# A recurrent attention kernel: the Q/K and V work of each segment in finer pieces, and the projections of the extra tokens in 32-column tiles

## The chip, the cores and the metric

The kernel runs on one core of a Trainium2 chip. The metric is the device time of the core in microseconds (us). A time quoted for a kernel is the median of its runs. A run counts as slow when it lies over 1.5% above the fastest run of the same kernel, and the state is unknown for a kernel that ran only once. The chip also reports the clock that its throttle granted to the matmul engine, as a share of full speed.

The names of the engines in the profile are PE (matmuls), PEld (the load of the stationary operand of a matmul, which PE overlaps with other matmuls), DVE (the vector engine), ACT (the scalar engine), POOL (a general engine) and SP (which issues DMAs).

## The reference, cut to what matters

```python
# x: 2048 tokens of 512; 64 segments of 32 tokens; H = 32 heads of Dh = 128; 8 memory rows
mem = mem0
for s in range(64):
    h = concat([mem, x[32*s : 32*s+32]])         # 40 rows (x is layer-normalized)
    q, k, v = h @ Wq, h @ Wk, h @ Wv             # per head
    p = softmax(where(mask, q k^T * scale, -1e9))
    o = (p v) @ Wo                               # 40 x 512
    mem = o[:8]                                  # the next segment waits for this
    outs.append(o[8:])
h  = x + concat(outs)
h2 = h + B(layernorm(h))                         # a gated MLP with a 2048 x 2048 mix over the tokens
```

The line `mem = o[:8]` makes the 64 segments a recurrence: a segment can't start its projections before the output projection of the one before it is done.

## The kernel before

The kernel has three parts. A prologue loads the weights, normalizes the first tokens and computes projections ("X" in what follows) of the first "extra" tokens. These are the eight tokens of each segment that do not fit into the 32-row tiles in which the recurrence works. The loop runs the 64 segments, and pours the X projections of later segments into gaps of PE. The tail is the gated MLP.

The parts that the change touches, shortened:

```python
# Q and K of a segment: 2 halves of 16 heads x (Q, K), each 16 matmuls of 512 columns in 32-column tiles
def QK(s, b, mi):
    for dc in range(4):
        for c in range(4):
            matmul(ps[32*c:32*c+32, bank, :], lhsT=hT[:, sl, dc, :], rhs=<512 columns of w_q or w_k>, tile_position=(0, 32*c))
def QK_evac(s, b, mi):                      # PSUM -> SBUF on ACT, then a 32x32 block transpose on DVE
    act(activation(out=Tst[:, mi, :], in_=ps[:, bank, :]))
    dve(transpose(out=QT or KT, in_=Tst[:, mi, :]))

# X projections of Q and K: 16 full-array matmuls (128 x 128 x 128) to a group of four heads
def qkx_mm(ck, i, bank):
    for hh in range(4):
        for dc in range(4):
            matmul(ps[:, bank, hh*128:(hh+1)*128], lhsT=ws[:, dc, h*128:(h+1)*128], rhs=hTe[:, ck % 3, dc, :])

# the two normalization products of a half, both on DVE
def sm_norm(b):
    dve(scalar_tensor_tensor(E_sb[:, b, 0:160], R_sb, RK, E_sb))
    dve(scalar_tensor_tensor(<the 64 extra columns>, R_sb, RK, <the same>))

# order of one segment
for b in range(2):
    for mi in range(2): QK(s, b, mi); QK_evac(s, b, mi)
S_half(s, 0); sm_exp(0); V_half(s, 0); V_evac(0, "dve"); sm_sums(0); sm_ln(0)
S_half(s, 1); sm_exp(1); sm_rcp(0)
V_half(s, 1, (0, 1, 2)); sm_sums(1); sm_ln(1); sm_rcp(1); V_half(s, 1, (3,)); V_evac(1, "act")
sm_norm(0); sm_norm(1)
<one X group: matmuls>                       # filler
PV_half(s, 0); PV_half(s, 1); <evict the four banks>
<eviction of the X group>
Wo(...)                                      # 32 matmuls of 384 columns, then 32 of 128 columns
mem_out(s)                                   # the 8 memory rows, back to the input of the next segment
# [cut: gap fillers, DMA, the tail]
```

S is the score product, PV the product of the probabilities and V, and Wo the output projection.

The softmax here doesn't subtract the row's maximum and nothing guards it: scores larger than these inputs give would overflow.

## Time and profile before

The kernel before took 933.24 us as the median of three runs (933.03 to 933.27).

| what | us | read from |
|---|---|---|
| span of the profiled run | 931.4 | the profile page |
| prologue, to the first Q/K matmul of segment 0 | 33.04 | the timeline of PE |
| one segment, without X filler | 10.90 | the timeline of PE |
| one segment, with X filler | 10.95 to 11.0 in most | the timeline of PE |
| from the last segment's start to the end | 193.0 | the timeline of PE |

This is PE in segment 48 of the kernel before. Each line gives the start, the length, the engine, the source line, the operation, the operands, the shape, how many instructions, and in brackets the idle time before it with what ended it. L475 is Q/K, L505 the first matmuls of S, L586 PV, L619 Wo.

```profile
574.80 3.64 PE L475 MATMUL f_ps<-f_arena,f_hT 128*32 128x512 bf16 x64 [0.32 <-ACT f_hT L641]
578.26 0.27 PE L505 MATMUL f_ps<-f_mask,f_ident 128*32 128x224 bf16 x4
...
579.50 0.27 PE L505 MATMUL f_ps<-f_mask,f_ident 128*32 128x224 bf16 x4
...
582.05 0.28 PE L586 MATMUL f_ps<-f_E_sb,f_V_sb 32*128 32x40 bf16 x16 [0.56 <-DVE f_E_sb L560]
...
582.90 1.93 PE L619 MATMUL f_ps<-f_arena,f_cT 128*32 128x384 bf16 x64
...
585.70 0.61 PE L475 MATMUL f_ps<-f_arena,f_hT 128*32 128x512 bf16 x8 [0.30 <-ACT f_hT L641]
```

From one Q/K to the next are 585.70 − 574.80 = 10.90 us, and these are the steps: 3.46 to the first S, 3.79 from there to the second PV, 0.85 to Wo, 2.80 to the next Q/K. Before the second PV, PE waits 0.56 us for DVE (line 560, the product of the extra columns). Before Q/K it waits 0.30 us for ACT. A segment that also carries X filler takes only some 0.05 us more, so the filler fills gaps, and the segment is a chain of latencies.

In the prologue PE computes the X projections. This is the group of these matmuls in the kernel before, from the page's list of groups. Its columns are the shape (partitions by elements) and the count, then the busy time and the mean ns of one instruction, then the idle time before them and what ended most of it.

```profile
L406 PE MATMUL f_ps<-f_hTe,f_arena 128*128 128x128 bf16 x1024 | 66.8, 223 | 1.5 <-ACT f_V_sb L576 1.0
```

1024 matmuls had 1.5 us of idle time before them in the whole run, none of it worth naming in the prologue.

### The profile page before, as it was taken

How to read it: one execution, taken by the hardware profiler on the slowest of the kernel's cores; microseconds unless marked ns; L12 is line 12 of the kernel's file. 1: busy time of each engine (PE TensorE's matmuls, PEld its weight loads, DVE VectorE, ACT ScalarE, POOL GpSimd, SP SyncE). 2: the span in 40 equal slices, each digit the busy share in tenths (PEclk: the TensorE clock that was granted, in tenths of full speed). 3: DMA queues.
4: the chain of work that ended last, by engine and by line, in shares of the span. 5: the costliest groups of instructions: out<-in, count | busy, mean ns of one | idle time of the engine just before them, and what ended most of it. 6: DMA issues, size and time to landing. Idle time of an engine off the chain costs nothing.

```text
span 931.4 us, 45500 instructions
## 1 busy us (share of the span) xinstructions
PE 885.5 (95%) x20973; PEld 486.4 (52%) x20973; DVE 448.0 (48%) x1034; ACT 475.4 (51%) x1153; POOL 112.5 (12%) x280
## 2 busy tenths in 40 slices
PE   7979999999999999999999999998999999989998
PEld 6644555555555555555555555454444444444443
DVE  3434555555454555554545555444444464453434
ACT  2435666666565666666565656565656565500000
POOL 1511111111111111111101111111101022200000
PEclk9989999999999999999999999999999999999999
DMA  9952222122203211221213020413121292021201
GB/s 329 376 141 56 66 53 65 35 49 63 71 19 74 45 53 40 53 60 38 65 32 65 32 67 20 116 31 77 37 54 49 72 284 98 1 91 46 89 14 36
DMA packets 103380, 71.29 MB, mean 77 GB/s; under 512 B 62120, under 2 KB 88688, under 8 KB 103184
## 3 DMA queue, kind: packets, MB, share of 16 engines
q1 hardware_dynamic: 102672, 68.06, 25.8%
q8 instruction: 166, 2.72, 1.2%
q14 instruction: 30, 0.25, 0.1%
q0 software_dynamic: 192, 0.20, 0.1%
q10 hardware_dynamic: 320, 0.07, 0.0%
HBM read 39.46 MB, written 18.61 MB: 62 GB/s over the span
## 4 chain that ended last, share of the span: by engine, by line
PE 91%; ACT 4%; DVE 2%; issue 1%; DMA 1%; SPq 0%; POOL 0%
PE f_ps L475 25%; PE f_ps L619 13%; PE f_ps L569 11%; PE f_ps L1016 10%; PE f_ps L406 6%; PE f_ps L663 4%; PE f_ps L586 3%; PE f_ps L978 3%; PE f_ps L1009 3%; PE f_ps L1086 2%; PE f_ps L638 2%; PE f_ps L425 2%; PE f_ps L514 2%; ACT f_hT L641 1%; PE f_ps L535 1%
## 5 line engine op out<-in xcount | busy, mean ns | idle before, releaser
L475 PE MATMUL f_ps<-f_arena,f_hT 128*32 128x512 bf16 x4096 | 233.0, 380 | 10.5 <-ACT f_hT L641 8.0
L482 ACT ACTIVATE f_Tst<-f_ps 128x512 bf16<-128x512 f32 x256 | 152.8, 597 | 110.7 <-PE f_ps L475 110.1
L475 PEld LDWEIGHTS f_ps<-f_arena,f_hT 128*32 128x32 bf16 x4096 | 103.6, 97 | 122.0 <-ACT f_hT L641 24.1
L488 DVE STREAM_TRANSPOSE f_QT<-f_Tst 128x256 uint32<-128x256 uint32 x128 | 57.0, 445 | 176.6 <-ACT f_Tst L482 176.6
L569 PE MATMUL f_ps<-f_arena,f_hT 128*32 128x512 bf16 x2048 | 139.9, 378 | 0.0
L619 PE MATMUL f_ps<-f_arena,f_cT 128*32 128x384 bf16 (+1 forms) x4096 | 125.4, 275 | 2.4 <-ACT f_cT L605 2.1
L619 PEld LDWEIGHTS f_ps<-f_arena,f_cT 128*32 128x32 bf16 x4096 | 84.9, 97 | 61.0 <-ACT f_cT L605 31.4
L1016 PE MATMUL f_ps<-f_arena 128*128 128x512 bf16 x448 | 101.3, 379 | 2.5 <-DVE f_arena L1022 1.6
L631 ACT ACTIVATE f_part<-f_ps 128x384 bf16<-128x384 f32 (+1 forms) x128 | 46.4, 384 | 75.4 <-PE f_ps L619 75.4
L491 DVE STREAM_TRANSPOSE f_KT<-f_Tst 128x256 uint32<-128x256 uint32 x128 | 57.0, 445 | 52.8 <-ACT f_Tst L482 52.7
L607 DVE TENSOR_SCALAR f_cT<-f_ps 128x320 bf16<-128x320 f32 x128 | 56.9, 487 | 42.4 <-PE f_ps L592 42.4
L498 POOL COPY f_QT<-f_arena 128x256 bf16<-128x256 bf16 x64 | 30.8, 481 | 357.7 <-PE f_ps L520 357.6
L1016 PEld LDWEIGHTS f_ps<-f_arena 128*128 128x128 bf16 x448 | 43.5, 98 | 55.9 <-DVE f_arena L1022 2.6
L605 ACT ACTIVATE f_cT<-f_ps 128x320 bf16<-128x320 f32 x128 | 49.0, 435 | 39.4 <-PE f_ps L592 39.4
L406 PE MATMUL f_ps<-f_hTe,f_arena 128*128 128x128 bf16 x1024 | 66.8, 223 | 1.5 <-ACT f_V_sb L576 1.0
L406 PEld LDWEIGHTS f_ps<-f_hTe,f_arena 128*128 128x128 bf16 x1024 | 59.4, 100 | 11.2 <-issue 9.8
L555 DVE SCALAR_TENSOR_TENSOR f_E_sb<-f_R_sb,f_E_sb 128x160 bf16<-128x160 f32 x128 | 41.7, 326 | 46.0 <-ACT f_R_sb L551 46.0
L547 ACT ACTIVATE f_R_sb<-f_ps 128x160 f32<-128x160 f32 x128 | 38.8, 303 | 37.4 <-PE f_ps L540 37.4
L569 PEld LDWEIGHTS f_ps<-f_arena,f_hT 128*32 128x32 bf16 x2048 | 44.4, 95 | 21.8
L627 POOL COPY f_cTx<-f_cT 128x256 bf16<-128x256 bf16 x64 | 26.1, 408 | 196.8 <-DVE f_cT L607 196.8
L1022 DVE TENSOR_TENSOR f_arena<-f_ps,f_arena 128x512 f32<-128x512 f32 x28 | 19.3, 691 | 57.8 <-PE f_ps L1016 57.8
L586 PE MATMUL f_ps<-f_E_sb,f_V_sb 32*128 32x40 bf16 x2048 | 36.5, 178 | 10.5 <-DVE f_E_sb L560 9.0
(103 smaller groups left out, 1092.5 us busy)
## 6 DMA issues: line engine op xcount, KB each, us to landing
wT_d<-f_wst SPq DMA_DIRECT2D x32, 256.0 KB, 2.4
f_arena<-wT_d SPq DMA_DIRECT2D x32, 256.0 KB, 4.7
f_arena<-in_A_Wq_dram SPq DMA_DIRECT2D x4, 1024.0 KB, 9.7
f_arena<-in_A_Wk_dram SPq DMA_DIRECT2D x4, 1024.0 KB, 14.0
f_arena<-in_A_Wv_dram SPq DMA_DIRECT2D x4, 1024.0 KB, 14.5
f_arena<-in_A_Wo_dram SPq DMA_DIRECT2D x4, 1024.0 KB, 13.5
f_Vx<-vext_d SPq DMA_DIRECT2D x62, 64.0 KB, 2.5
vext_d<-f_Vs SPq DMA_DIRECT2D x24, 128.0 KB, 2.1
```

Source lines behind the costliest of these rows:

```text
L406: pe(lambda e, h=h, dc=dc, hh=hh: e.matmul(ps[:, bank, hh * 128:(hh + 1) * 128], lhsT=ws[:, dc, h * DH:(h + 1) * DH], rhs=hTe[:, ck % 3, d ...
L475: pe(lambda e, dc=dc, c=c, rhs=rhs: e.matmul(ps[32 * c:32 * c + 32, bank, :], lhsT=hT[:, sl, dc, :], rhs=rhs, start=(dc == 0), stop=(dc == ...
L482: act(lambda e: e.activation(out=Tst[:, tb, :].rearrange("p (hp i r) -> p hp i r", i=32, r=2), in_=ps[:, bank, :].rearrange("p (hp r i) -> ...
L488: dve(lambda e: e.transpose(out=dst, in_=src), reads=[("T", tb)], writes=[("QT", b)])
L491: dve(lambda e: e.transpose(out=dst, in_=src), reads=[("T", tb)], writes=[("KT", b)])
L569: pe(lambda e, dc=dc, c=c, c0=c0: e.matmul(ps[32 * c:32 * c + 32, bank, :], lhsT=hT[:, sl, dc, :], rhs=w_v[:, dc, c0:c0 + 512], start=(dc ...
L586: pe(lambda e, q=q, c=c, g=g, c0=c0: e.matmul(ps[:, PVB[c], c0:c0 + 40], lhsT=V_sb[q, b, g * 128:(g + 1) * 128], rhs=E_sb[q, b, g * 40:(g ...
L605: act(lambda e: e.activation(out=dst, in_=src, func=ACT.Copy, scale=UNSC), reads=[PB(PVB[c])], writes=[("cT", c)])
L607: dve(lambda e: e.tensor_scalar(out=dst, in0=src, scalar1=UNSC, scalar2=None, op0=ALU.mult), reads=[PB(PVB[c])], writes=[("cT", c)])
L619: pe(lambda e, h=h, g=g, i=i, b=b, c=c: e.matmul(ps[32 * g:32 * g + 32, bank, 0:d1 - d0], lhsT=cTh[:, i, 8:40], rhs=w_o[:, h, d0:d1], star ...
L631: act(lambda e: e.activation(out=part[:, s % 8, d0:d1], in_=ps[:, bank, 0:d1 - d0], func=ACT.Copy), reads=[PB(bank)], writes=[("part", s % ...
L1016: pe(lambda e: e.matmul(ps[:, bank, 0:TB], lhsT=z2[:, sc, fb * 128:(fb + 1) * 128], rhs=wTb[tb % 2][:, :, sc, :], start=(sc == 0), stop=(s ...
```

## The change

Its intent is to shorten the chain from Q/K to the second PV.

- The second half of Q and K comes in two 8-head pieces, so that the last eviction and transpose before the second S are half as long.
- The second half of V goes to two PSUM banks, each evicted on its own, one by DVE and one by ACT.
- The second S moves ahead of the sums of the first half and of the last quarter of V.
- The product of the extra columns moves from DVE to Pool, beside the other product.
- The X projections of Q and K use four 32-column tiles instead of the full array, so that PE does not change its mode between them and the matmuls of the segment. The first half of an X group goes before PV and the second half behind `mem_out`. One filler of V moves ahead of Wo.

The core of the diff, with cuts at "...":

```diff
-    def qkx_mm(ck, i, bank, only_hh=None, only_dc=None):
+    def qkx_mm(ck, i, bank, hhs=range(4)):
 ...
-                pe(lambda e, h=h, dc=dc, hh=hh: e.matmul(ps[:, bank, hh * 128:(hh + 1) * 128], lhsT=ws[:, dc, h * DH:(h + 1) * DH],
-                                                         rhs=hTe[:, ck % 3, dc, :], start=(dc == 0), stop=(dc == DC - 1)),
+                for c in range(4):
+                    q = slice(32 * c, 32 * c + 32)
+                    pe(lambda e, h=h, dc=dc, hh=hh, c=c, q=q: e.matmul(
+                        ps[q, bank, hh * 128:(hh + 1) * 128], lhsT=ws[:, dc, h * DH + 32 * c:h * DH + 32 * c + 32],
+                        rhs=hTe[:, ck % 3, dc, :], start=(dc == 0), stop=(dc == DC - 1), tile_position=(0, 32 * c)),
 ...
-    QKB = {(0, 0): 0, (0, 1): 1, (1, 0): 6, (1, 1): 7}
+    QKP = ((0, 0, 8, (0, 1)), (1, 0, 4, (6, 7)), (1, 4, 4, (3, 2)))     # (half, first pair, pairs, banks of Q and K)
-    VB = (6, 2)
+    VB = {(0, 0): 6, (1, 0): 2, (1, 1): 7}
 ...
     def sm_norm(b):
-        dve(lambda e: e.scalar_tensor_tensor(out=ev, in0=rv, scalar=RK, in1=ev, op0=ALU.mult, op1=ALU.mult),
+        pool(lambda e: e.tensor_tensor(out=ev, in0=rv, in1=ev, op=ALU.mult),
 ...
-        V_half(s, 0)
-        V_evac(0, "dve")
-        sm_sums(0)
-        sm_ln(0)
+        V_half(s, 0, (0, 1, 2))
         S_half(s, 1)
+        sm_sums(0)
         sm_exp(1)
+        sm_ln(0)
+        V_half(s, 0, (3,))
+        V_evac(0, "dve")
 ...
-        V_half(s, 1, (0, 1, 2))
+        V_half(s, 1, gs=(0, 2))
+        V_evac(1, "dve", (0, 2))
         sm_sums(1)
+        sm_rcp(0)
         sm_ln(1)
         sm_rcp(1)
-        V_half(s, 1, (3,))
-        V_evac(1, "act")
+        V_half(s, 1, gs=(2, 4))
+        V_evac(1, "act", (2, 4))
 ...
-        ev = [gx.pop(0)()] if gx else []
+        xs = gx.pop(0) if gx else []
+        for f in xs[:2]:
+            f()
         PV_half(s, 0)
         PV_half(s, 1)
 ...
-        late = []
+        late = gv.pour(1)
         Wo((0, 2, 1, 3), OB, 0, OC)
 ...
             mem_out(s)
-        late += gv.pour(1)
+        for f in xs[2:]:
+            f()
```

The scale constants of the softmax change too (a factor moved from one product into the eviction of V), and some groups of matmuls take another PSUM bank.

More of the change, by code (lines that the diff above doesn't have):

```diff
@@ L191, in fast_path @@
     NEG = -1.0e30
-    RBIAS = 44.42
+    RBIAS = 44.24
     LNS = 2.0 ** -64
-    RK = math.exp(-RBIAS)
+    VSC = 2.0 ** -64
     em = Emitter(n_dma_sems=40)
@@ L395, in mem0_transpose @@
         act(lambda e: e.activation(out=hT[:, 0, :, 0:M], in_=src, func=ACT.Copy), reads=[PB(bank)], writes=[("hTm", 0)])
-    def qkx_mm(ck, i, bank, only_hh=None, only_dc=None):
+    def qkx_mm(ck, i, bank, hhs=range(4)):
         mi, h0 = i // 8, 4 * (i % 8)
         ws = (w_q, w_k)[mi]
-        for hh in range(4):
+        for hh in hhs:
             h = h0 + hh
             for dc in range(DC):
-                if only_hh is not None and (hh, dc) != (only_hh, only_dc):
-                    continue
-                pe(lambda e, h=h, dc=dc, hh=hh: e.matmul(ps[:, bank, hh * 128:(hh + 1) * 128], lhsT=ws[:, dc, h * DH:(h + 1) * DH],
-                                                         rhs=hTe[:, ck % 3, dc, :], start=(dc == 0), stop=(dc == DC - 1)),
-                   reads=[("hTe", ck % 3), ("W", mi, h // 8)], writes=[PB(bank)])
+                for c in range(4):
[3 more added lines that the diff above has]
+                        rhs=hTe[:, ck % 3, dc, :], start=(dc == 0), stop=(dc == DC - 1), tile_position=(0, 32 * c)),
+                        reads=[("hTe", ck % 3), ("W", mi, h // 8)], writes=[PB(bank)])
     def qkx_evac(ck, i, bank, eng="act"):
@@ L436, in vx_evac @@
         if eng == "act":
-            act(lambda e: e.activation(out=t, in_=ps[:, bank, :], func=ACT.Copy), reads=[PB(bank)], writes=tok)
+            act(lambda e: e.activation(out=t, in_=ps[:, bank, :], func=ACT.Copy, scale=VSC), reads=[PB(bank)], writes=tok)
         else:
-            dve(lambda e: e.tensor_copy(out=t, in_=ps[:, bank, :]), reads=[PB(bank)], writes=tok)
+            dve(lambda e: e.tensor_scalar(out=t, in0=ps[:, bank, :], scalar1=VSC, scalar2=None, op0=ALU.mult), reads=[PB(bank)], writes=tok)
         b, c = n // 4, n % 4
@@ L464, in fast_path, with QK @@
     OB2 = 0
+    FBK = 7
     OC = 384
     VXB = 5
-    def QK(s, b, mi):
+    def QK(s, piece, mi):
+        b, p0, np_, banks = piece
         ws = (w_q, w_k)[mi]
-        bank = QKB[(b, mi)]
+        bank = banks[mi]
         sl = slot(s)
+        h0, nh = 16 * b + 2 * p0, 2 * np_
         for dc in range(DC):
             for c in range(4):
-                rhs = ws[:, dc, :].rearrange("p (h c i) -> p c h i", c=4, i=32)[:, c, 16 * b:16 * b + 16, :]
-                pe(lambda e, dc=dc, c=c, rhs=rhs: e.matmul(ps[32 * c:32 * c + 32, bank, :], lhsT=hT[:, sl, dc, :], rhs=rhs,
+                rhs = ws[:, dc, :].rearrange("p (h c i) -> p c h i", c=4, i=32)[:, c, h0:h0 + nh, :]
+                pe(lambda e, dc=dc, c=c, rhs=rhs: e.matmul(ps[32 * c:32 * c + 32, bank, 0:32 * nh], lhsT=hT[:, sl, dc, :], rhs=rhs,
@@ L476, in QK, with halves @@
                                                            start=(dc == 0), stop=(dc == DC - 1), tile_position=(0, 32 * c)),
                    reads=[("hTx", (s // 4) % 3), ("hTm", s), ("W", mi, 2 * b), ("W", mi, 2 * b + 1)], writes=[PB(bank)])
-    def QK_evac(s, b, mi):
-        bank = QKB[(b, mi)]
-        tb = mi
-        act(lambda e: e.activation(out=Tst[:, tb, :].rearrange("p (hp i r) -> p hp i r", i=32, r=2),
-                                   in_=ps[:, bank, :].rearrange("p (hp r i) -> p hp i r", r=2, i=32), func=ACT.Copy),
-            reads=[PB(bank)], writes=[("T", tb)])
-        src = Tst[:, tb, :].bitcast(U32)
-        if mi == 0:
-            dst = QT[:, b, :, :, :].rearrange("p hp q r -> p (hp q r)").bitcast(U32).rearrange("p (hp q) -> p hp q", hp=8)[:, :, 8:40]
-            dve(lambda e: e.transpose(out=dst, in_=src), reads=[("T", tb)], writes=[("QT", b)])
-        else:
-            dst = KT[:, b, :, :, :].rearrange("p hp q r -> p (hp q r)").bitcast(U32)
-            dve(lambda e: e.transpose(out=dst, in_=src), reads=[("T", tb)], writes=[("KT", b)])
+    def halves(b, p0, np_):
+        return range(p0 // 4, (p0 + np_) // 4)
@@ new lines, in QK_evac @@
+    def QK_evac(piece, mi):
+        b, p0, np_, banks = piece
+        bank = banks[mi]
+        st_ = Tst[:, mi, 64 * p0:64 * (p0 + np_)]
+        tok = [("T", mi, k) for k in halves(b, p0, np_)]
+        act(lambda e: e.activation(out=st_.rearrange("p (hp i r) -> p hp i r", i=32, r=2),
+                                   in_=ps[:, bank, 0:64 * np_].rearrange("p (hp r i) -> p hp i r", r=2, i=32), func=ACT.Copy),
+            reads=[PB(bank)], writes=tok)
+        src = st_.bitcast(U32)
+        dt_, nm = ((QT, "QT"), (KT, "KT"))[mi]
+        dst = dt_[:, b, p0:p0 + np_, :, :].rearrange("p hp q r -> p (hp q r)").bitcast(U32)
+        if mi == 0:
+            dst = dst.rearrange("p (hp q) -> p hp q", hp=np_)[:, :, 8:40]
+        dve(lambda e: e.transpose(out=dst, in_=src), reads=tok, writes=[(nm, b, k) for k in halves(b, p0, np_)])
@@ L509, in S_half @@
         buf = (s // CK) % 2
-        rd = [("QT", b), ("KT", b), ("QTe", b)]
+        rd = [(n, b, k) for n in ("QT", "KT") for k in range(2)] + [("QTe", b)]
         for g in range(4):
@@ L554, in sm_norm @@
     def sm_norm(b):
-        dve(lambda e: e.scalar_tensor_tensor(out=E_sb[:, b, 0:160], in0=R_sb[:, b, :], scalar=RK, in1=E_sb[:, b, 0:160],
-                                             op0=ALU.mult, op1=ALU.mult),
+        dve(lambda e: e.tensor_tensor(out=E_sb[:, b, 0:160], in0=R_sb[:, b, :], in1=E_sb[:, b, 0:160], op=ALU.mult),
             reads=[("R", b), ("E", b)], writes=[("E", b)])
@@ L559, in sm_norm, with V_half, V_evac @@
         rv = R_sb[:, b, :].rearrange("p (g q) -> p g q", q=40)[:, :, 0:16]
-        dve(lambda e: e.scalar_tensor_tensor(out=ev, in0=rv, scalar=RK, in1=ev, op0=ALU.mult, op1=ALU.mult),
-            reads=[("R", b), ("Ex", b)], writes=[("Ex", b)])
-    def V_half(s, b, dcs=range(DC)):
-        bank = VB[b]
+        pool(lambda e: e.tensor_tensor(out=ev, in0=rv, in1=ev, op=ALU.mult),
+             reads=[("R", b), ("Ex", b)], writes=[("Ex", b)])
+    def V_half(s, b, dcs=range(DC), gs=(0, 4)):
+        bank = VB[b, gs[0] // 2]
         sl = slot(s)
+        w = 128 * (gs[1] - gs[0])
         for dc in dcs:
             for c in range(4):
-                c0 = (16 * b + 4 * c) * DH
-                pe(lambda e, dc=dc, c=c, c0=c0: e.matmul(ps[32 * c:32 * c + 32, bank, :], lhsT=hT[:, sl, dc, :], rhs=w_v[:, dc, c0:c0 + 512],
+                c0 = (16 * b + 4 * c + gs[0]) * DH
+                pe(lambda e, dc=dc, c=c, c0=c0: e.matmul(ps[32 * c:32 * c + 32, bank, 0:w], lhsT=hT[:, sl, dc, :], rhs=w_v[:, dc, c0:c0 + w],
                                                          start=(dc == 0), stop=(dc == DC - 1), tile_position=(0, 32 * c)),
                    reads=[("hTx", (s // 4) % 3), ("hTm", s), ("W", 2, 2 * b), ("W", 2, 2 * b + 1)], writes=[PB(bank)])
-    def V_evac(b, eng):
-        bank = VB[b]
+    def V_evac(b, eng, gs=(0, 4)):
+        bank = VB[b, gs[0] // 2]
+        dst, src = V_sb[:, b, 128 * gs[0]:128 * gs[1]], ps[:, bank, 0:128 * (gs[1] - gs[0])]
+        tok = [("V", b, g) for g in range(*gs)]
         if eng == "act":
-            act(lambda e: e.activation(out=V_sb[:, b, :], in_=ps[:, bank, :], func=ACT.Copy), reads=[PB(bank)], writes=[("V", b)])
+            act(lambda e: e.activation(out=dst, in_=src, func=ACT.Copy, scale=VSC), reads=[PB(bank)], writes=tok)
         else:
-            dve(lambda e: e.tensor_copy(out=V_sb[:, b, :], in_=ps[:, bank, :]), reads=[PB(bank)], writes=[("V", b)])
+            dve(lambda e: e.tensor_scalar(out=dst, in0=src, scalar1=VSC, scalar2=None, op0=ALU.mult), reads=[PB(bank)], writes=tok)
     def PV_half(s, b):
@@ L588, in PV_half @@
                     start=(g == 0), stop=False, skip_group_check=True, tile_position=(32 * c, 0)),
-                    reads=[("V", b), ("E", b)], writes=[PB(PVB[c])])
+                    reads=[("V", b, g), ("E", b)], writes=[PB(PVB[c])])
         for c in range(4):
@@ L596, in PV_half @@
                 reads=[("Vx", xb), ("Ex", b)], writes=[PB(PVB[c])])
-    UNSC = 2.0 ** -64
+    UNSC = math.exp(-RBIAS)
     def cT_evac(c, eng):
@@ L789, in qkx_group @@
     def qkx_group(ck, i):
-        def f():
-            qkx_mm(ck, i, XB)
-            return lambda: qkx_evac(ck, i, XB, "dve")
-        gx.append(f)
+        gx.append([lambda hh=hh: qkx_mm(ck, i, XB, (hh,)) for hh in range(4)] + [lambda: qkx_evac(ck, i, XB, "dve")])
     def vx_group(ck, n):
-        def f():
-            vx_mm(ck, n, XB)
-            return lambda: vx_evac(ck, n, XB, "dve")
-        gx.append(f)
+        gx.append([lambda dc=dc: vx_mm(ck, n, XB, dc) for dc in range(DC)] + [lambda: vx_evac(ck, n, XB, "dve")])
     def vx_atoms(ck, n):
@@ L846, in fast_path @@
             load_xe(3, 1)
-        for b in range(2):
+        for piece in QKP:
             for mi in range(2):
-                QK(s, b, mi)
+                QK(s, piece, mi)
                 lastop["qk"[mi]] = em.by_eng["pe"][-1]
-                QK_evac(s, b, mi)
+                QK_evac(piece, mi)
         if s == NSEG - 1:
@@ L874, in fast_path @@
                 xn2T_dma(r, [lastop["s"], lastop["x"]])
-        sm_rcp(0)
         if s == 0:
@@ L903, in fast_path @@
         cT_evac(3, "dve")
-        for f in ev:
-            f()
         if rb > 0:
@@ L916, in fast_path @@
         if j4 == 3 and rb > 0:
-            F_group(rb - 1, XB)
-            WoX_scatter(rb - 1, XB)
-            h_done(rb - 1, XB)
+            F_group(rb - 1, FBK)
+            WoX_scatter(rb - 1, FBK)
+            h_done(rb - 1, FBK)
         if j4 == 1 and 2 <= rb + 2 < RB:
@@ L926, in fast_path @@
         if j4 == 2 and 2 <= rb + 2 < RB:
-            xT(0, XB)
-            late.append(lambda: ring_copy(rb + 2, XB))
+            xT(0, FBK)
+            late.append(lambda: ring_copy(rb + 2, FBK))
         if s == 9:
-            xT(1, XB)
-            late.append(lambda: xe_copy(3, XB))
+            xT(1, FBK)
+            late.append(lambda: xe_copy(3, FBK))
         if s + 1 < NSEG:
             mem_out(s)
-        late += gv.pour(1)
+        for f in xs[2:]:
+            f()
         for f in late:
```

## The prediction

> **What bounds the kernel.** The page has PE busy 95%, but that is not a throughput bound. The trace shows 64 recurrent segments, each starting with the Q/K projection (line 475). Their periods are 10.90 to 11.0 us, whether a segment carries X-projection filler (10.95 at segment 32) or none (10.90, segments 48 to 62). So filler is nearly free, and the segment is a chain of latencies. From the timeline: Q/K projection 3.46 us; from there to the second PV half 3.79 (3.84 with full-array X filler); PV to the output projection 0.845 (line 605's eviction); output projection 1.71; its end to the next Q/K 1.09 (evict, mem_out, evict). 63 segments make about 690 of 931 us; some 60 before and 190 after are hardly touched.
>
> **What the change does to each term.**
> 1. Q/K to second PV. Before, S of the second half waits for the last K transpose: a 128x512 eviction (0.597) and a 128x256 transpose (0.445) put its matmuls 1.35 us after the Q/K end. In half pieces I estimate 0.38 and 0.30 (fits over the sizes the trace shows), so they start at about 1.0; twelve V matmuls fill that. exp then starts near 1.35 instead of 1.74. The sums now come behind a V quarter and half (near 1.89, not 2.15), ln/exp end near 2.90 (was 3.17). Before, the second PV waited for a 0.58 us V eviction and two DVE products in series (3.53 and 3.66). Now the eviction is a half, the ext product is on Pool, and the DVE product ends near 3.26. But V's last part sits in bank 7, which PV writes: PV waits for that eviction, near 3.2. Second PV near 3.45: minus 0.34.
> 2. X in column tiles: four 32-column N=128 matmuls take 56 ns in the output projection, as one 128x128x128 does now, so no throughput gain. What goes is the change of array mode: 313 instead of 216 ns from V to X. The Trainium skill, "TensorEngine Tiling (Array Packing)", Key Properties, says changing tiling mode drains the array; the trace agrees. Worth 0.04 to 0.08 where X is present.
> 3. A V-filler quarter (0.216) before the output projection: 0.435+0.216 of PE against the 0.845 wait: plus 0.05 in some 35 segments. X's second half (0.45) fits behind mem_out (0.48 us to the next Q/K).
> 4. More, smaller matmuls (2.5 ns per group of four): plus 0.02.
>
> Sum: 0.28 to 0.36 per segment, period about 10.62; times 63 is 17 to 22 us. The prologue has four times the X matmuls at the same pace: no change.
>
> **Prediction.** 915 us, range 904 to 926 (8 in 10). Faster by over 2%: 0.48; within 2%: 0.50; slower: 0.02.
>
> **What would show it.** Period near 10.6 with X and 10.57 without; second S about 1.0 us after the Q/K end; second PV near 3.45; PV to output projection 0.84 to 0.90; last two terms unchanged; no step longer than 216 ns between the last V and X; prologue still about 33 us; DVE loses 28 us of ext products, Pool gains 128.
>
> **What would make it wrong.** (a) Pool's ext product slower than my 0.35 us estimate, or blocked by DVE: "SBUF — State Buffer", Who interferes with whom, says a two-input DVE instruction contends with a Pool instruction that reads SBUF, and the DVE product and ext product would run together; the trace has no such pair. Then the second PV's closing matmuls wait and up to 0.2 us goes back. (b) DVE, with two V evictions before the first product, binds instead. (c) The bank-7 wait puts both PV halves later than 3.45. (d) Four times the PE instructions in the prologue starve its instruction fetch (plus a few us). (e) If small evictions and transposes are cheaper than fitted, the gain is larger, to 28 us.

## More of the kernel before

Every matmul that the kernel issues becomes two instructions of PE: one that loads the stationary operand and one that multiplies.

Lines of the profile page of the kernel before follow. The first is the span, the second is each engine's busy time with its share of the span and its number of instructions. The third is the DMA queue that brings instructions, with its packets, megabytes and share of the 16 DMA engines. The last is the share of each engine in the chain of waits that ended last.

```profile
span 931.4 us, 45500 instructions
...
PE 885.5 (95%) x20973; PEld 486.4 (52%) x20973; DVE 448.0 (48%) x1034; ACT 475.4 (51%) x1153; POOL 112.5 (12%) x280
...
q8 instruction: 166, 2.72, 1.2%
...
PE 91%; ACT 4%; DVE 2%; issue 1%; DMA 1%; SPq 0%; POOL 0%
```

A reader would take from "PE 95%" that PE is the limit. The timeline of a segment says otherwise.

## The result, and the profile after

| kernel | median, us | range, us | runs |
|---|---|---|---|
| before | 933.25 | 933.03 to 933.71 | 4 |
| after | 1013.39 | 1010.23 to 1021.59 | 4 |

The kernel after is slower: the ratio is 1.0871, with a 95% interval of 1.0805 to 1.0938. Here and below, a ratio is the mean time of one kernel's fast runs over that of the kernel before in the same rounds, so it is not quite the ratio of the medians quoted. All results were correct.

These are the same lines of the profile page for the kernel after, with the line of its X matmuls from the list of groups.

```profile
span 1009.7 us, 57985 instructions
...
PE 898.9 (89%) x27110; PEld 594.8 (59%) x27117; DVE 461.2 (46%) x1098; ACT 462.8 (46%) x1281; POOL 155.5 (15%) x408
...
q8 instruction: 214, 3.51, 1.5%
...
PE 86%; issue 8%; DVE 3%; ACT 2%; DMA 1%; POOL 0%; POOLq 0%; ACTq 0%
...
L406 PE MATMUL f_ps<-f_hTe,f_arena 128*32 128x128 bf16 x4096 | 87.4, 236 | 35.6 <-issue 35.4
```

The chain of waits now has "issue" at 8% against 1%. "Issue" is time in which an engine waited for nothing that the profile shows. The X matmuls are four times as many, and 35.4 us of "issue" lie before them. PE and PEld together have 12,281 more instructions. The instruction queue brought 214 packets instead of 166. Each packet has 16,384 bytes in the trace, and each holds 256 instructions, that is up to 128 pairs of load and matmul: the batches below show it, and in all ten runs of this document the trace has 254 PE and PEld records for each packet.

The waits of PE in the kernel after, from the view of waits, the largest first: what waited, for what, the us in total, how often, and the longest.

```profile
PE f_ps L406 <- issue: 35.4, 23, 4.5
PE f_ps L578 <- issue: 9.2, 11, 1.6
PE f_ps L597 <- issue: 8.6, 12, 1.7
PE f_ps L630 <- issue: 8.4, 15, 1.4
```

All the waits of PE in this view that end in "issue" sum to 74.7 us, against 0.6 us in the kernel before and a loss of 78.3 us in the span. In the kernel before, the largest waits of PE were of another kind:

```profile
PE f_ps L586 <- DVE f_E_sb L560: 9.0, 16, 0.6
PE f_ps L475 <- ACT f_hT L641: 8.0, 26, 0.3
```

What such a stop looks like is seen in the prologue. This is PE's timeline in the kernel after.

```profile
15.39 1.97 PE L406 MATMUL f_ps<-f_hTe,f_arena 128*32 128x128 bf16 x128 [3.22 <-issue]
21.86 3.60 PE L406 MATMUL f_ps<-f_hTe,f_arena 128*32 128x128 bf16 x127 [4.50 <-issue]
28.69 3.61 PE L406 MATMUL f_ps<-f_hTe,f_arena 128*32 128x128 bf16 x128 [3.23 <-issue]
...
59.99 1.97 PE L406 MATMUL f_ps<-f_hTe,f_arena 128*32 128x128 bf16 x128 [1.24 <-issue]
```

For comparison, a stretch of the same work in the prologue of the kernel before:

```profile
20.92 3.76 PE L406 MATMUL f_ps<-f_hTe,f_arena 128*128 128x128 bf16 x64 [0.17 <-DMA f_arena<-in_A_Wk_dram]
```

In the kernel after, PE runs 128 matmuls (127 in the second batch; all 1536 X matmuls of the prologue are on record, so none is missing there), stops, and runs 128 again: one block of 256 instructions at a time. Inside the first batch the pace is good: 128 in 1.97 us are 62 ns for a set of four tiles, the fill and drain of the batch included. The blocks simply come only every 6.5 to 6.8 us.

The windows of the same stretches show what else happens. The columns are the window and its length, then busy time and count for PE, PEld, DVE, ACT and POOL, then the granted clock, the busy share of the DMA engines and their GB/s.

```profile
15.30:21.80 6.50, 1.97 (x128) 1.79 (x128) 0.69 (x1) 0.60 (x1) 0.00 (x0) 0.91 1.06 374
21.80:28.60 6.80, 3.60 (x127) 3.34 (x128) 0.69 (x1) 0.60 (x1) 0.00 (x0) 0.50 1.05 387
182.00:375.00 193.00, 176.90 (x6512) 127.58 (x6512) 93.87 (x237) 105.40 (x306) 31.22 (x80) 1.00 0.20 48
```

The DMA engines are full of weights. During the second stop, at 20.6 us, the granted clock falls to 0.50, and a batch takes 3.60 instead of 1.97 us. That costs little here, because the batches start 6.5 to 6.8 us apart with either clock. In the loop (the last window) the clock is 1.00 and the DMA engines are mostly idle.

In the loop the stops are shorter and fall anywhere. These are pieces of the chain of waits in one segment of the kernel after, in order of time: start, us, and what.

```profile
431.40 0.11 PE f_ps L406 x8
431.51 0.86 issue
432.37 0.52 PE f_ps L406 x24
...
434.05 1.58 PE f_ps L630 x52
435.63 1.44 issue
437.07 0.38 PE f_ps L630 x12
```

PE stops for 0.86 us in the middle of an X group and for 1.44 us in the middle of Wo, where no operand is missing: the stop comes after 52 of its 64 matmuls, and the last 32 read the four tiles that the first 32 had already read.

Yet the chain of latencies did get shorter. Segment 58, which carries no X, gives this timeline in the kernel after (L480 is Q/K, L514 the first matmuls of S, L597 PV, L630 Wo):

```profile
753.80 3.66 PE L480 MATMUL f_ps<-f_arena,f_hT 128*32 128x512 bf16 x96 [0.30 <-ACT f_hT L652]
757.28 0.27 PE L514 MATMUL f_ps<-f_mask,f_ident 128*32 128x224 bf16 x4
...
758.15 0.27 PE L514 MATMUL f_ps<-f_mask,f_ident 128*32 128x224 bf16 x4
...
760.71 0.27 PE L597 MATMUL f_ps<-f_E_sb,f_V_sb 32*128 32x40 bf16 x15
...
761.57 1.93 PE L630 MATMUL f_ps<-f_arena,f_cT 128*32 128x384 bf16 x64
...
764.37 0.40 PE L480 MATMUL f_ps<-f_arena,f_hT 128*32 128x512 bf16 x4 [0.30 <-ACT f_hT L652]
```

The two products of the extra columns on Pool, from the timeline of all engines in the same segment:

```profile
759.67 0.31 POOL L568 TENSOR_TENSOR f_E_sb<-f_R_sb,f_E_sb 128x64 bf16<-128x64 f32 x1 [7.63 <-ACT f_R_sb L560]
...
760.32 0.38 POOL L568 TENSOR_TENSOR f_E_sb<-f_R_sb,f_E_sb 128x64 bf16<-128x64 f32 x1 [0.34 <-ACT f_R_sb L560]
```

| step, us | before, segment 48 | after, segment 58 | predicted |
|---|---|---|---|
| Q/K to first S | 3.46 | 3.48 | +0.02 |
| first S to second S | 1.24 | 0.87 | |
| first S to second PV | 3.79 | 3.43 | 3.45 |
| second PV to Wo | 0.85 | 0.86 | 0.84 to 0.90 |
| Wo to the next Q/K | 2.80 | 2.80 | unchanged |
| period | 10.90 | 10.57 | 10.57 |

So the time went elsewhere. Where it went is worked out from the starts of the segments in the two profiled runs:

| part | before, us | after, us | difference |
|---|---|---|---|
| prologue | 33.04 | 68.91 | +35.9 |
| segment 0 | 26.32 | 24.64 | −1.7 |
| segments 1 to 47 | 515.44 | 563.05 | +47.6 |
| segments 48 to 62 | 163.58 | 160.61 | −3.0 |
| segment 63 and the tail | 193.00 | 192.47 | −0.5 |
| span | 931.4 | 1009.7 | +78.3 |

Almost all the loss is in the parts that have tiled X work: the prologue, and segments 8 to 47 (segments 1 to 7, without it, take 11.00 us against 10.95; segments 14 and 15, which have none either, take 10.88 and 10.62).

### The profile page after: what moved, and what is told of

Read it like the earlier page. It is cut to its first block, busy times and chain, and to the rows that moved or that the text cites. A ratio compares the mean times of both kernels' runs of the same rounds, so it can differ in the third digit from the quotient of the medians.

```text
span 1009.7 us, 57985 instructions
## 1 busy us (share of the span) xinstructions
PE 898.9 (89%) x27110; PEld 594.8 (59%) x27117; DVE 461.2 (46%) x1098; ACT 462.8 (46%) x1281; POOL 155.5 (15%) x408
## 4 chain that ended last, share of the span: by engine, by line
PE 86%; issue 8%; DVE 3%; ACT 2%; DMA 1%; POOL 0%; POOLq 0%; ACTq 0%
PE f_ps L480 23%; PE f_ps L630 12%; PE f_ps L578 10%; PE f_ps L1024 9%; PE f_ps L406 7%; PE f_ps L674 3%; PE f_ps L597 3%; PE f_ps L426 3%; PE f_ps L986 2%; PE f_ps L1017 2%; PE f_ps L1094 2%; PE f_ps L649 2%; PE f_ps L523 2%; DVE f_V_sb L589 2%; PE f_ps L514 1%
## 5 line engine op out<-in xcount | busy, mean ns | idle before, releaser
L480 PE MATMUL f_ps<-f_arena,f_hT 128*32 128x512 bf16 (+1 forms) x6144 | 238.0, 309 | 5.2 <-ACT f_hT L652 4.6
L492 ACT ACTIVATE f_Tst<-f_ps 128x256 bf16<-128x256 f32 (+1 forms) x384 | 156.9, 453 | 103.2 <-PE f_ps L480 84.6
L480 PEld LDWEIGHTS f_ps<-f_arena,f_hT 128*32 128x32 bf16 x6144 | 162.9, 97 | 67.9 <-ACT f_hT L652 9.4
L578 PE MATMUL f_ps<-f_arena,f_hT 128*32 128x256 bf16 (+1 forms) x3072 | 144.3, 308 | 9.2 <-issue 9.2
L630 PE MATMUL f_ps<-f_arena,f_cT 128*32 128x384 bf16 (+1 forms) x4096 | 130.3, 275 | 9.3 <-issue 8.4
L630 PEld LDWEIGHTS f_ps<-f_arena,f_cT 128*32 128x32 bf16 x4096 | 89.1, 97 | 63.8 <-ACT f_cT L616 22.6
L406 PE MATMUL f_ps<-f_hTe,f_arena 128*32 128x128 bf16 x4096 | 87.4, 236 | 35.6 <-issue 35.4
L500 DVE STREAM_TRANSPOSE f_QT<-f_Tst 128x128 uint32<-128x128 uint32 (+1 forms) x192 | 65.9, 343 | 75.9 <-ACT f_Tst L492 75.4
L406 PEld LDWEIGHTS f_ps<-f_hTe,f_arena 128*32 128x32 bf16 x4096 | 73.5, 106 | 41.1 <-issue 40.2
L589 DVE TENSOR_SCALAR f_V_sb<-f_ps 128x512 bf16<-128x512 f32 (+1 forms) x128 | 65.8, 554 | 55.4 <-PE f_ps L578 55.4
L500 DVE STREAM_TRANSPOSE f_KT<-f_Tst 128x128 uint32<-128x128 uint32 (+1 forms) x192 | 68.5, 357 | 47.5 <-ACT f_Tst L492 46.8
L578 PEld LDWEIGHTS f_ps<-f_arena,f_hT 128*32 128x32 bf16 x3072 | 71.3, 96 | 26.2 <-issue 13.2
L537 ACT ACTIVATE f_E_sb<-f_ps 128x224 bf16<-128x224 f32 x128 | 45.4, 355 | 36.8 <-PE f_ps L529 35.6
L597 PE MATMUL f_ps<-f_E_sb,f_V_sb 32*128 32x40 bf16 x2048 | 42.4, 178 | 17.2 <-issue 8.6
L597 PEld LDWEIGHTS f_ps<-f_E_sb,f_V_sb 32*128 32x128 bf16 x2048 | 28.3, 91 | 36.1 <-DVE f_E_sb L564 14.5
```

Of the source, the lines that this page charges most:

```text
L406: pe(lambda e, h=h, dc=dc, hh=hh, c=c, q=q: e.matmul(ps[q, bank, hh * 128:(hh + 1) * 128], lhsT=ws[:, dc, h * DH + 32 * c:h * DH + 32 * c ...
L480: pe(lambda e, dc=dc, c=c, rhs=rhs: e.matmul(ps[32 * c:32 * c + 32, bank, 0:32 * nh], lhsT=hT[:, sl, dc, :], rhs=rhs, start=(dc == 0), sto ...
L492: act(lambda e: e.activation(out=st_.rearrange("p (hp i r) -> p hp i r", i=32, r=2), in_=ps[:, bank, 0:64 * np_].rearrange("p (hp r i) -> ...
L500: dve(lambda e: e.transpose(out=dst, in_=src), reads=tok, writes=[(nm, b, k) for k in halves(b, p0, np_)])
L578: pe(lambda e, dc=dc, c=c, c0=c0: e.matmul(ps[32 * c:32 * c + 32, bank, 0:w], lhsT=hT[:, sl, dc, :], rhs=w_v[:, dc, c0:c0 + w], start=(dc ...
L589: dve(lambda e: e.tensor_scalar(out=dst, in0=src, scalar1=VSC, scalar2=None, op0=ALU.mult), reads=[PB(bank)], writes=tok)
```

## The experiments

**Theory.** PE is short of instructions. They come in blocks of 256, and the queue needs a minimum time for a block: some 6.5 us while weights fill the DMA engines, some 3.8 us otherwise. A segment whose chain is shorter than 3.8 us for each 256 of its PE instructions must become longer than its chain.

**Rivals.** (1) The column-tiled X matmuls are themselves slow, or make others wait. (2) The new order or the shared banks make waits: X is split around PV and uses bank 3, where a piece of Q now lands, and PV waits for bank 7. (3) The throttle: the lower clock is a cause and not a result. (4) The loss in the prologue has a cause of its own there.

Rival 1 already stands badly, as the pace inside a batch is as good as was hoped. The starts of the instruction packets in the DMA records give the first measure of the theory (us from the start of the span):

```
before   17.0  25.0  31.8  38.6  45.2  50.8                    loop: one every 4.4 (median)
after    13.0  19.4  26.1  32.5  39.0  46.1  49.9  53.7  57.5  61.1  65.0  68.9
                                                               loop: one every 3.8 (median), 3.3 at least
```

Each packet itself took about 1.1 us, so the interval is not the transfer of the 16 KiB alone. The packets and the stops belong together: each of the eleven batches that follow a stop in the prologue of the kernel after starts 2.4 to 2.8 us after the start of a packet. In the kernel after, the interval is 6.4 to 7.1 us while weights load (to about 47 us) and 3.8 us from then on. Before the first segment, 408 matmuls run in the kernel before and 1560 in the kernel after. The extra 1152 are nine blocks of 128 pairs.

### X back on the full array, everything else as in the kernel after

```diff
-                for c in range(4):
-                    matmul(ps[q, bank, ...], lhsT=ws[:, dc, h*DH + 32*c : h*DH + 32*c + 32], ..., tile_position=(0, 32*c))
+                matmul(ps[:, bank, ...], lhsT=ws[:, dc, h*DH:(h+1)*DH], ...)
```

> The changed kernel with only the X projections of Q and K put back to full-array 128x128x128 matmuls (16 a group instead of 64); everything else of the change stays. Theory A (PE is starved of instructions: its fetch brings 256 of them per 3.5 to 6.5 us): start of the first segment back near 33 us (69 in the changed kernel), no stops of 1 to 4 us after every 128th matmul, segments with X near 10.65 us instead of 12.2, time about 915 (910 to 922). Rival B (what is slow is the rest of the change in segments that carry X: pouring, banks, DVE and Pool together): segments with X stay above 11.5 us, time above 955.

Measured: 931.68 us (931.24 to 933.91), ratio 0.9977 (0.9957 to 0.9997), with 190 instruction packets. The first segment starts at 32.90 us. So undoing the tiles alone takes back 1013.39 − 931.68 = 81.7 us, of which 36.0 in the prologue. Rival 2 falls as the main cause: the order, the banks and the split of X around PV are all still in.

But the forecast of some 915 us was missed. The segments without X took 10.67 us and those with X 11.0 us. Two reasons are in the trace. Q, K and V in smaller pieces are still 96 more PE instructions in each segment, and 20 waits for "issue", 8.4 us in all, are still there. And the array mode changes twice behind `mem_out` again: from the end of Wo to the next Q/K are 1.27 us, where the kernel after has 1.09 (medians), in the 38 segments with X, some 7 us in all. One of the waits for "issue", in the middle of the last V matmuls of a segment:

```profile
372.80 0.40 PE L575 MATMUL f_ps<-f_arena,f_hT 128*32 128x256 bf16 x8 [0.39 <-issue]
```

### X in two 64-column tiles: twice the matmuls instead of four times

```diff
-                for c in range(4):
-                    q = slice(32*c, 32*c + 32)      # tile_position=(0, 32*c)
+                for c in range(2):
+                    q = slice(64*c, 64*c + 64)      # tile_position=(0, 64*c)
```

> The changed kernel with the X projections of Q and K in two 64-column tiles (32 matmuls a group) instead of four 32-column ones. Array time per group is the same 0.9 us by the pace rule seen (56 ns per set of tiles). Theory A: half the instructions, so between: first segment starts at 40 to 50 us, segments with X 10.7 to 11.2 us, time 925 to 940. Rival C (column tiling as such is slow, not the number of instructions): like the changed kernel, first segment near 65 to 70 us, time above 990.

Measured: 953.11 us (952.53 to 954.30), ratio 1.0206 (1.0189 to 1.0223), with 198 packets. The first segment starts at 45.05 us, within the forecast. The segments with X took 11.14 us, also within their forecast, yet the time is 13 us above the upper end of its own: the longer prologue (12.0 us) and segments 1 to 47 (8.9 us more than before) add up to more than the forecast of the time had allowed. PE's timeline in its prologue:

```profile
17.14 3.76 PE L406 MATMUL f_ps<-f_hTe,f_arena 128*64 128x128 bf16 x128 [0.62 <-issue]
23.61 5.25 PE L406 MATMUL f_ps<-f_hTe,f_arena 128*64 128x128 bf16 x127 [2.71 <-issue]
```

The batches are again 128 matmuls, and they start 23.61 − 17.14 = 6.47 us apart, as in the kernel after, though the tiles are twice as wide and the work of a batch takes twice as long. The size of the batch follows the count of instructions and not the work in it.

### The tiles alone, in the kernel before

The edit is the reverse of the first experiment, in the kernel before: only `qkx_mm` has the four tiles.

> The kernel before with only the X projections of Q and K in four 32-column tiles. Theory A: first segment starts near 69 us (plus 36); segments with X have about 720 PE instructions, some 2.8 fetches of 3.6 us, so about 11.0 to 11.4 us (10.95 before); time 970 to 990. Rival B: the loop has none of the pouring and banks, so only the prologue could suffer, and if fetch is not the cause not even that: time within 10 us of 933.

Measured: 985.07 us (981.69 to 986.35), ratio 1.0539 (1.0511 to 1.0567). The first segment starts at 68.28 us (68.91 in the kernel after), and the segments with X take 11.53 us, a little above the forecast. The rest of the change is absent, and the loss in the prologue is whole. This is the complement of the first experiment: the tiles are sufficient for it, and necessary.

### Matmuls that compute nothing, where PE would be idle

The kernel before, with tiny matmuls (8 columns, results unused) in its last segments, which have no X: none to segment 50, 48 a segment in 51 to 54, and 128 a segment from 55 on.

```diff
+    def dummies(n):
+        for i in range(n):
+            c = i % 4; q = slice(32*c, 32*c + 32)
+            matmul(ps[q, VXB, 0:8], lhsT=ident[:, q], rhs=ident[:, 0:8], tile_position=(0, 32*c))
 ...
+        dose = 0 if s < 51 else 48 if s < 55 else 128
+        dummies(min(dose, 48))                 # before PV
 ...
+        dummies(24 if dose > 48 else 0)        # before Wo
 ...
+            dummies(56 if dose > 48 else 0)    # behind mem_out
```

> The kernel before with extra 8-column matmuls in the late segments that have no X filler, placed where PE idles: none in segments 48 to 50, 48 in 51 to 54, 128 in 55 to 62. They need 6 ns of array each, at most 0.8 us against 1.2 us of idle time. Theory A: none 10.90 us; 48 (some 680 instructions a segment, 2.65 fetches) no change, 10.90 to 10.95; 128 (some 840, 3.3 fetches of 3.5 to 3.7 us) 11.5 to 12.3 us, time 938 to 945. Rival (only array time and waits count): 10.9 to 11.15 in all, time 933 to 935.

Measured: 956.73 us (955.66 to 959.95), ratio 1.0252 (1.0227 to 1.0277). The periods from segment 48 on, in us:

```
none:    10.91 10.91 10.91
48:      10.93 10.91 11.28 10.91
128:     12.01 11.58 16.51 11.65 11.86 12.08 14.49 11.20
```

In themselves the tiny matmuls were about as short as forecast (steps of 6 to 8 ns in most groups). 48 pairs cost nothing in three segments of four; 128 cost from 0.3 to 5.6 us a segment. The stops look like those of the kernel after. Two are shown: one in the middle of the tiny matmuls, and one in the middle of Q/K, whose operands had all arrived.

```profile
675.78 1.05 PE L475 MATMUL f_ps<-f_arena,f_hT 128*32 128x512 bf16 x16
678.25 4.36 PE L475 MATMUL f_ps<-f_arena,f_hT 128*32 128x512 bf16 x48 [1.42 <-issue]
...
690.01 0.45 PE L836 MATMUL f_ps<-f_ident 128*32 128x8 bf16 x38
692.17 0.28 PE L836 MATMUL f_ps<-f_ident 128*32 128x8 bf16 x18 [1.71 <-issue]
```

The direction was forecast, the size (938 to 945 us) was not. Two things were missing from the forecast. First, the granted clock dropped to 0.50 twice, from 678.1 us in segment 57 (16.51 us long) and from 766.8 us in segment 63. The first drop set in at a stop for instructions: the 48 matmuls of Q/K behind it took 4.36 us, where 64 usually take 3.64. Second, DMA traffic comes in bursts here too: segment 61 (14.49 us) had its full clock, and the DMA engines were 0.84 busy in the 3 us around its first stop, as they were 0.68 busy at the stop in segment 57.

So rival 3 has a share: a stretch at half clock can come with a stop for instructions, and the two are then added. But it comes second, as the other seven segments were longer by 0.3 to 3.6 us with no such drop.

### Fewer instructions: one Q piece, full-array X

The first experiment, with the second half of Q in one piece again; K, whose transpose comes last, stays in two. That is 16 pairs less a segment.

```diff
-    QKP = ((0, 0, 8, (0, 1)), (1, 0, 4, (6, 7)), (1, 4, 4, (3, 2)))
+    QKP = (((0,0,8,(0,1)),0), ((0,0,8,(0,1)),1), ((1,0,8,(6,6)),0), ((1,0,4,(7,7)),1), ((1,4,4,(2,2)),1))
 ...
-        for piece in QKP:
-            for mi in range(2):
+        for piece, mi in QKP:
```

> The full-array X version with the second half of Q in one piece again and only its K in two: 16 matmuls, 32 PE instructions fewer a segment. The last K piece, for which S waits, is as early as before. Theory A (instruction fetch): about 692 instructions in a segment with X, 2.7 fetches of 3.8 us = 10.3 us, against a chain of 10.57: fewer stops, segments with X 10.65 to 10.85 (11.0 in the full-array X version), time 916 to 926. If what lengthens those segments is not the instruction count but pouring, banks or array mode, they stay at 11.0: time 930 to 933.

Measured: 922.91 us (921.10 to 925.32), ratio 0.9889 (0.9870 to 0.9908), within the forecast. Segments without X took 10.57 us, and most of those with X 10.77. So it gains over the kernel before, and what separates it from the first experiment is 16 pairs a segment. The banks differ too, as Q's last piece no longer lands in bank 3; but that had cost nothing, since Q/K took 3.48 us to the first S in every segment 8 to 47 of the first experiment, against 3.47 here. The waits for "issue" fell from 8.4 to 1.6 us. In segment 20 the step from the end of Wo to the next Q/K is 1.27 us instead of 1.09: the two quarters of X behind `mem_out` (0.45 us of work) and two changes of the array mode fit no longer into the wait for ACT.

### The same, with V's second half in one bank

```diff
-        V_half(s, 1, gs=(0, 2)); V_evac(1, "dve", (0, 2))
+        V_half(s, 1, (0, 1))
         sm_sums(1); sm_rcp(0); sm_ln(1); sm_rcp(1)
-        V_half(s, 1, gs=(2, 4)); V_evac(1, "act", (2, 4))
+        V_half(s, 1, (2, 3)); V_evac(1, "act")
```

> As b1, and the second V half again as one piece of 512 columns in one bank, evicted by ACT: another 16 matmuls fewer, about 660 instructions with X and 615 without, 2.6 fetches of 3.8 us = 9.9 us. The chain loses little (V's eviction ends about 0.15 us later, but PV no longer waits for bank 7): 10.60 to 10.75 without X, 10.65 to 10.80 with X and hardly a stop. Theory A: time 914 to 922. Rival: as for b1, 930 or more.

Measured: 926.46 us (925.36 to 928.03), ratio 0.9925 (0.9909 to 0.9940), above the forecast. Another 16 pairs are saved, but the second PV comes 3.53 us after the first S instead of 3.42 (segment 20), so this time fewer instructions did not win: at 661 a segment, the chain decides and not the supply. The change of array mode behind `mem_out` (1.27 us again) was not counted in the forecast either.

### The weights of V and Wo loaded later

The kernel after, with the loads of Wv, and of Wo behind them in the queue, held back until the last X matmul of the prologue. It tests whether the DMA traffic sets the 6.5 us interval.

```diff
+    xdone = [<the last X matmul of the prologue>]
-        load_w(2, hq)
+        load_w(2, hq, after=xdone)
```

> The changed kernel, but the load of Wv (and with it Wo, behind it in the queue) waits for the last prologue X matmul, so the DMA engines fall quiet at about 28 us instead of 47. Theory A with fetch time set by the DMA traffic: the fetches come every 6.5 us until about 28 us and then every 3.6 to 3.9, the first segment starts at 57 to 61 us (69); segment 0 is longer by 5 to 10 us for the late Wv, so the whole time moves little (1000 to 1020). If the 6.5 us of the prologue belong to its instruction mix and not to the DMA traffic, fetches stay at 6.5 us up to 47 us and the first segment starts near 69.

Measured: 998.72 us, one run, so its state is unknown. The first segment starts at 57.77 us, within the forecast, 11.1 us earlier than in the kernel after. Segment 0 is 8.6 us longer, as forecast; the whole time came out just under its forecast of 1000 to 1020 us. The windows of its prologue, with the columns of above:

```profile
12.00:28.00 16.00, 7.68 (x314) 6.98 (x303) 1.38 (x2) 1.79 (x3) 0.00 (x0) 0.79 0.98 356
28.00:58.00 30.00, 19.44 (x1089) 17.27 (x1092) 8.81 (x17) 6.33 (x12) 10.63 (x42) 0.94 0.02 5
```

Once the DMA engines were quiet (share 0.02), the packets came 3.3 to 3.8 us apart, where the kernel after had 6.4 to 7.1 until 46 us:

```
after                                    26.1  32.5  39.0  46.1  49.9  53.7  57.5  61.1  65.0  68.9
weights of V and Wo later                25.9  29.6  33.3  37.0  40.4  43.7  47.5  51.1  54.7  58.0
```

So the traffic of weights nearly doubles the time to fetch a block, and rival 4 falls: the prologue has the same cause as the loop, with a slower supply. The kernel after shows the same within its own prologue: 7.1 us to the packet at 46.1 us, 3.8 to the next, when the weights were in. In the loop (segments 16 to 36) the period was 11.89 us, against 12.28, with the same 3.19 packets a segment, so a packet took 3.7 us instead of 3.8. That difference is not explained; the four runs of the kernel after alone lie 11.4 us apart.

### Three quarters of X before PV, one behind

```diff
-        for f in xs[:2]:
+        for f in xs[:3]:
             f()
 ...
-        for f in xs[2:]:
+        for f in xs[3:]:
             f()
```

This is applied to the kernel with one Q piece and full-array X.

> b1 with three quarters of each X group before PV and one behind mem_out, instead of two and two. In b1 the two full-array quarters behind mem_out with their two changes of array mode take the last term from 1.09 to 1.27 us; one quarter should fit (0.22 us plus two changes of 0.1, against 0.48). Before PV, 12 full-array matmuls take 0.67 plus 0.19, so the first PV half moves from 3.10 to about 3.3 and the second from 3.42 to 3.45 to 3.55. Segments with X 10.60 to 10.70 (10.76 in b1), time 916 to 921. If the array-mode account is wrong, 922 to 926.

Measured: 920.61 us (919.66 to 921.76), ratio 0.9864 (0.9847 to 0.9880). It beats both kernels, the one before by 1.4%. From the page of this kernel:

```profile
span 918.1 us, 49665 instructions
...
q8 instruction: 182, 2.98, 1.4%
```

In segment 20, Wo's end to the next Q/K is 1.09 us again, and the second PV comes 3.47 us after the first S; most segments with X take 10.65 us, those without 10.57. PE's timeline shows the X matmuls behind `mem_out` and before PV:

```profile
468.84 0.40 PE L404 MATMUL f_ps<-f_hTe,f_arena 128*128 128x128 bf16 x4
...
475.23 0.84 PE L404 MATMUL f_ps<-f_hTe,f_arena 128*128 128x128 bf16 x12
```

### All kernels beside each other

The count is of PE and PEld records in the trace between the starts of segments 16 and 37 (all of which have X) and between 49 and 63 (none). The packets are those of the instruction queue in the same stretch, and the last column is the period over the packets.

| kernel | segments | PE instructions a segment | packets a segment | period, us | us a packet |
|---|---|---|---|---|---|
| before | 49 to 63 | 583 | 2.21 | 10.91 | 4.9 |
| before | 16 to 37 | 629 | 2.48 | 10.97 | 4.4 |
| Q piece whole, X three to one | 49 to 63 | 646 | 2.50 | 10.57 | 4.2 |
| V whole too | 16 to 37 | 661 | 2.57 | 10.89 | 4.2 |
| after | 49 to 63 | 678 | 2.64 | 10.61 | 4.0 |
| Q piece whole, X three to one | 16 to 37 | 692 | 2.71 | 10.79 | 4.0 |
| Q piece whole | 16 to 37 | 692 | 2.71 | 10.88 | 4.0 |
| full-array X | 16 to 37 | 724 | 2.81 | 11.01 | 3.9 |
| before, with tiles | 16 to 37 | 725 | 2.81 | 11.53 | 4.1 |
| two 64-column tiles | 16 to 37 | 756 | 2.95 | 11.14 | 3.8 |
| after | 16 to 37 | 820 | 3.19 | 12.28 | 3.8 |

With more instructions the time for a packet falls to 3.8 us and no further (3.7 in the single run with the weights later, which is not in the table). From there the period grows with the count: with the 3.8 us of the prologue, 820/256 × 3.8 = 12.2 us, and 12.28 were measured. Below it the chain decides. Between the two, how the instructions are spread seems to matter: "full-array X" and "before, with tiles" have the same count, yet 11.01 and 11.53 us. In the latter the 128 instructions of an X group stand in one place and run in about 1 us, while a block takes 3.8 us to come; that explanation was argued and not tested by itself.

The waits of PE for "issue" go the same way. Their sums in the profiled runs are 0.6 us before, 74.7 after, 43.3 with the tiles alone, 19.4 with two tiles, 8.4 with full-array X, 1.6 with Q whole, 1.2 with V whole too and 4.0 with X three to one.

## Why the prediction was wrong, and where it was right

**What was right.** The reading that the segment is a chain of latencies, and the terms of that chain, as the segments without X show. The second PV was predicted 3.45 us after the first S and came at 3.43; the period without X was predicted as 10.57 and was 10.57 (segment 58). The 256-column eviction was estimated at 0.38 us and took 0.381. Of the risks, (a) did not come true in any size that mattered: the product on Pool took 0.31 us, and 0.38 where it ran beside DVE's product for most of its length, against the 0.35 of the estimate. (b) and (c) did not either, as the second PV was on time. (e) did not. Item 3, a V filler before Wo for 0.05 us, was about right: in segments with X the step from PV to Wo was 0.90 to 0.91 us in the kernels with full-array X, against 0.85.

**The step that failed.** Item 2 said "four 32-column N=128 matmuls take 56 ns in the output projection, as one 128x128x128 does now, so no throughput gain", and from it the prediction drew: "The prologue has four times the X matmuls at the same pace: no change." The time of execution was right: a batch of 128 ran in 1.97 us. What failed is the step from "the same time of execution" to "no change". Each matmul is two instructions that must first arrive. Four times as many at 56 ns a set need a block of 256 every 1.8 us (128 pairs are 32 sets of 56 ns), while the queue brought one every 3.8 us, or every 6.5 us under the traffic of weights. In the kernel before, the full-array matmuls take 56 ns for each pair (107 in the first 4 us of them), so a block lasts 7.2 us, a little over the 6.5 us of a fetch. Hence the supply stayed hidden; the prologue was close to the limit and its profile showed nothing of it.

**A term mis-sized.** Risk (d) named the very mechanism, "Four times the PE instructions in the prologue starve its instruction fetch", and sized it "plus a few us". It measured plus 35.9 us. It could have been bounded from the profile of before: its packets came 6.8 us apart while the weights loaded (25.0, 31.8, 38.6), each for a block that PE was done with in about that time. That nine more blocks might need as much again, 61 us, was there to be asked; the trace of before alone could not say how much less it would be.

**A term left out.** The same limit in the loop. The prediction charged the extra matmuls 0.02 us a segment for their execution. In segments 16 to 36, 820 instructions a segment need 3.2 blocks and 12.28 us, where the chain would need about 10.6. Segments 8 to 47 took 47.2 us more than before, nearly all of the +47.6 us of segments 1 to 47. So the gain on the chain was real and is paid out only where there is no X (−3.0 us in segments 48 to 62), and the kernel with fewer instructions collects it.

**The Trainium skill on this.** "Runtime: NRT & Kernel Launch", section Instruction fetch mechanics, says that instruction memory is refilled in blocks of 256 instructions while the engine executes the current one, and that the cost of crossing a block is "mostly hidden". The size of the block agrees with the traces (packets of 16,384 bytes, batches of 128 pairs, 254 counted instructions a packet). That it is hidden holds for the kernel before, and not for the kernel after, whose waits for "issue" sum to 74.7 us of the 78.3 us lost.

"TensorEngine Tiling (Array Packing)", section Key Properties, says that a change of the tiling mode drains the array. The traces agree: two quarters of X behind `mem_out` put the next Q/K 1.27 us after the end of Wo on the full array, and 1.09 us in 32-column tiles (medians). The step from `mem_out` to X is 112 ns instead of 29, and that from X to Q/K 149 instead of 54. So the intent of the tiles was sound, but what they save, 0.18 us at that place, is about a tenth of what their instructions cost in a segment (12.28 − 10.6 = 1.7 us).

**What stays open.** How the drop of the clock and the stop for instructions belong together is seen only in part. The stops do not need the low clock: the first two of the prologue came while batches ran at full pace, and from 182 to 375 us the clock was 1.00 through all stops. And the drop comes with a stop of another kind too: in the kernel before, the clock was 0.50 from 53.1 to 59.9 us, and PE waited for a DMA from 51.0 to 53.9 us. But with the first stop of the prologue, of 3.22 us, there came no drop, and with one of 1.42 us elsewhere there came one, so what decides it stays open. And why a fetch takes 3.8 us when its packet takes 1.1 us is not visible in the trace.

## What to carry to other kernels

Before you split a matmul into smaller ones, count instructions and not only execution time: divide the instructions of the engine in the critical stretch by 256 and multiply by the interval between instruction packets that the trace shows when the engine is hungry (here 3.8 us, and 6.5 us while DMA is saturated). If that comes near the length of the stretch, the split costs what it was meant to save. Where it does, split only the piece whose latency ends the chain (here K, and not Q), and leave filler in the largest instructions; this gave 920.61 us, where all the splits together gave 1013.39 and the kernel before 933.25. An engine that the profile calls 89% busy may still be waiting for its program; the sign is "issue" before instructions whose operands are long there, in batches of a constant count.

## What the Trainium skill lacked or had wrong

- "Runtime: NRT & Kernel Launch", section Instruction fetch mechanics, calls the fetch mostly hidden and gives no rate. The runs show one block of 256 PE instructions every 3.8 us (3.3 at least) with quiet DMA, and every 6.4 to 7.1 us with 349 to 387 GB/s of weight traffic. A kernel above that rate lost 8.7%.
- The same section gives PE room for 2048 instructions. The trace shows no such reserve in use: in the kernel after, PE had executed 449 recorded instructions when the first packet of the queue started, it had stopped 0.8 us before, and from then on it ran one block and stopped.
- "TensorEngine Tiling (Array Packing)" says, in Key Properties, that a change of the mode drains the array, but nothing of what it costs to fetch the instructions of the tiles. Four tiles in place of one matmul were four times the PE instructions, 1152 more matmuls in the prologue, and +35.9 us.
- "TensorE: Matmul & The Clock Gate", section Back-to-back issue gap, gives about 81 ns for a sustained matmul of 128 columns in a stream with its loads. The full-array stream in the prologue of the kernel before ran at 56 ns (median step; 64 in 3.76 us, with the drain of the last one).
- The same page, Part 1, has the clock at half after an idle window of about 3.4 us. The traces agree only in part. In the prologue of the kernel after, the clock fell to 0.50 at 20.6, 41.1 and 47.9 us, in stops of 4.50, 3.28 and 3.75 us; but not in the first stop, of 3.22 us, and at 65.0 us it fell after one of 1.92. In the experiment with the tiny matmuls it fell at 678.1 us, in a stop of 1.42 us.
- "SBUF — State Buffer", section Who interferes with whom, has a Pool instruction that reads SBUF contend with a two-input DVE instruction, without the size for this pair. Here the Pool product took 0.31 us alone and 0.38 where DVE's product overlapped it by 0.22 us.
